# A shorter load list ahead of an attention and state-space kernel: two chunks first, the rest behind the small transfers

## The chip, the cores and the metric

One core of a Trainium2 chip runs the kernel. The metric is the device time of one execution in microseconds. Before the change it was 1209.28 us (median of 3 runs, 1208.81 to 1212.46). The engines named below: PE is TensorE with its weight loads (PEld), DVE is VectorE, ACT is ScalarE, POOL is GpSimd, SP is SyncE, which here only issues DMAs.

## What is computed

Two independent halves, joined along the last axis. A is a state-space convolution (S4) of 576 channels with 128 complex states each, over 2048 positions; B is attention with 32 query heads of 18 columns and a single shared key and value head.

```python
# A: K[d, l] = Re sum_n C[d, n] * exp(dt[d] * A[d, n] * l) * dt[d] * B[d, n]
P = jnp.exp(logdA[:, :, None] * l[None, None, :])
K = jnp.einsum("dn,dnl,dn->dl", Cc, P, dB).real
y = irfft(rfft(pad(u)) * rfft(pad(K)))[..., :L] + u * Dskip
# B: x is [1, 2048, 576], 32 heads of 18
q = (x @ wq).reshape(B, S, H, Dh).transpose(0, 2, 1, 3)
k, v = x @ wk, x @ wv
p = softmax(einsum("bhqd,bkd->bhqk", q, k) * Dh ** -0.5)
out = einsum("bhqk,bkd->bhqd", p, v).reshape(B, S, H * Dh) @ wo
```

## The kernel before

**Attention.** The 2048 positions are four chunks of 512 (`CT`). Keys are used as columns of `kaug` (128 partitions x 2048): for each of two heads a band of 55 rows, the high part of the key twice, its low part between, and a row of ones. Queries of two heads stand the same way in one of five `aug` tiles. One *pair* (line 478, `scores`) is a block of 128 keys against 512 queries of two heads: two matmuls into a score tile `s`, of which three exist. Line 489 takes the exponential of such a tile (128x1024) on ScalarE into one of eight `P` tiles; `product` (line 779) multiplies two of them with the values `v_sb` into `ops`. `main` (line 726) issues pairs in rounds of three (`NS`), all on the order of chunk, group of four heads, block of keys, pair of heads. Pairs 0 to 7 use the keys of chunk 0, 8 to 15 those of chunk 1, and so on; pair 32 is the first of the second group and needs the heads 4 and 5, pair 33 the heads 6 and 7. From the twelfth block of keys on, `force` makes sure that the aug tile of the next group has been asked for.

**Side work.** `side` (line 654) computes the other queries: `qproj` (line 366) for each chunk and each of five column blocks `wq[m]`, its high and low parts stored to DRAM (`qd`) from POOL and fetched from there into aug tiles by SP. `queries` for block 0 of chunk 0 comes first; it stores heads 4 to 7 out of the setup's `keys` tile (`store_first`). `prepare` and the output projections follow for each chunk.

**Convolution.** `Conv` works on 12 chunks of 48 channels. `front(k)` makes the kernel: `arguments` (line 1003) multiplies the parameters `raw` with exp(`dt`), makes the phase f and the exponent m (128x1248 each) and reduces the phase; `factors` (line 1051) takes the sines of f and of |f| (as a cosine) and the exponential of m; `tables` and `kgen` make 2048 positions out of them. Sine and exponential stand in different tables of ScalarE, so each run of sines inside the loop costs two table loads. Such a *burst* is shared by two chunks: the second one's factors go to DRAM (`kept`, tile `fr`) and come back (`restore`). `back(k)` transforms and multiplies. The generators are advanced by a planner with its own clock `K` (estimated times of PE, VectorE and ScalarE): `fill` puts their steps into the gaps of the attention, and `settle` (line 334) sets that clock behind the setup.

**The order.** On PE, ScalarE and VectorE the instructions run in the order in which the program emits them; DMAs go out in the order of emission on each issuing engine. A wait of one instruction therefore holds everything behind it on its engine.

**The setup** (line 222). SP issues dt0 and raw0 (parameters of convolution chunk 0, line 986), wkv, the five loads of chunk 0 of x (`x0`, line 255), then five of 384 or 768 KB for chunks 1 to 3 (`xr`, line 260), and wq1. `conv.begin(n)` advances `front(0)` by n steps. PE projects the queries of 96 columns and the keys of chunk 0 into `first` (line 280); ScalarE copies it (`h1`), VectorE takes the maximum `ab` and the remainder `l1`; SP and POOL place them into kaug and into the first two aug tiles by small transfers of 18 rows. `rest` projects the keys of chunks 1 to 3 and all values. `small`, `kmax`, `aw` and `bias` make the bound that the first group's exponentials subtract (L494 instead of L496).

Of the kernel before, what the change touches and what calls it, by code (L numbers as in the profile page):

```python
# [9 lines left out]
F32 = mybir.dt.float32  # L10
F32R = mybir.dt.float32r
# [173 lines left out]
class Attention:  # L185
# [36 lines left out]
    def setup(self, tp, conv):  # L222
# [13 lines left out]
        wkv = tp.tile([P, 5, 64], F32, name="wkv_sb")  # L236
        xr = tp.tile([P, 5, 3, CT], F32, name="xr")
# [5 lines left out]
        h1, l1, h2, l2, vt = (self.keys[:, j, :] for j in range(5))  # L243
        self.x0 = x0 = self.xp.tile([P, 5, CT], F32, name="x0", tag="x")

        nc.gpsimd.memset(x0[64:, 4, :], 0.0)
        nc.gpsimd.memset(xr[64:, 4], 0.0)
        for j in range(2):
            nc.gpsimd.memset(self.ring[j].bitcast(F32), 0.0)
        conv.early()  # L250
        nc.scalar.dma_start(self.wq[0], a["wq"][0])
        nc.sync.dma_start(wkv, a["wkv"])
        for k in range(5):
            n = DT[k][1]
            nc.sync.dma_start(x0[:n, k, :], a["xT"][0, :n, k, :])
# [8 lines left out]
        self.load_wq(1)  # L264
# [7 lines left out]
        self.todo, self.busy, self.group = [], False, 0  # L272
        self.side_work = Stream(self.side(), self.k, 99.0)
        conv.begin(6)
        p1, small = (self.ps_s.tile([P, 2, CT], F32, tag="s", name=n)[:, 0, :] for n in ("first", "small"))
        p2 = self.bank(CT, "second")
        pv = self.ps_o.tile([P, CT], F32, tag="o", name="vps")

        def queries(ps, j, k):
            nc.tensor.matmul(ps[32 * j:32 * j + 32, :], self.wq[0][:, k, 32 * j:32 * j + 32], x0[:, k, :],  # L280
                             start=(k == 0), stop=(k == 4), tile_position=(0, 32 * j))

        def project(ps, j, i, c, k):
            nc.tensor.matmul(ps[32 * j:32 * j + 32, :], wkv[:, k, i:i + 32], xr[:, k, c - 1, :] if c else x0[:, k, :],
                             start=(k == 0), stop=(k == 4), tile_position=(0, 32 * j))

        def rest(k):
            for c in range(1, NCH):
                project(p2, c - 1, 0, c, k)
            queries(p2, 3, k)  # L290
            for c in range(NCH):
                project(pv, c, 32, c, k)
# [8 lines left out]
        self.place(0, h1, l1, 96, (nc.sync, nc.sync))  # L301
        for pr in range(2):
            for row, src in ((0, h1), (18, h1), (36, l1)):
                for j in range(2):
                    h, b = 2 * pr + j, 64 * j + row
                    q = nc.sync if pr and row == 36 else nc.gpsimd
                    q.dma_start(self.aug[pr][b:b + 18, :].bitcast(F32), src[h * DH:h * DH + DH, :].bitcast(F32))
        V.tensor_scalar(self.km[:, 0:1], ab[:, 0:1], spread[:, 139:140], None, op0=ALU.mult)
        conv.begin(4)
        rest(0)  # L310
        nc.tensor.matmul(small[:, 0:1], spread[:, 0:128], self.km[:, 0:1], start=True, stop=True)
        V.tensor_copy(self.kmax[:, 0:1], small[:, 0:1])
        aw = self.p2.tile([P, P], F32, tag="aw", name="aw_first")
        V.tensor_scalar(aw, ab[:, 0:1].broadcast_to([P, P]), self.kmax[:, 0:1], 1.002, op0=ALU.mult, op1=ALU.mult)
        rest(1)
        matmul4(nc, small[:, 8:12], aw, self.sel[:, 0:4])
        V.tensor_reduce(self.bias, small[:, 8:12], axis=AX.X, op=ALU.max)
        V.tensor_scalar(self.bias, self.bias, -SCALE, None, op0=ALU.mult)
        for k in range(2, 5):
            rest(k)  # L320
        V.tensor_copy(h2, p2)
        V.tensor_tensor(l2, p2, h2.bitcast(F32), op=ALU.subtract)
        self.place(1, h2, l2, 0, (nc.sync, nc.gpsimd))
        V.tensor_copy(vt.bitcast(F32), pv)
        V.tensor_reduce(self.km[:, 4:5], p2, axis=AX.X, op=ALU.max, apply_absolute_value=True)
        self.vt = vt.bitcast(F32)

    def place(self, c, hi, lo, i, qs):
        for row, t in ((0, hi), (36, hi), (18, lo)):
            for j in range(2):  # L330
                b = 64 * j + row
                qs[j].dma_start(self.kaug[b:b + 18, c * CT:(c + 1) * CT].bitcast(F32), t[i:i + 18, :].bitcast(F32))

    def settle(self, conv):
# [3 lines left out]
        h2, l2 = self.keys[:, 2, :], self.keys[:, 3, :]  # L338
        vp = self.bank(CT, "vp").rearrange("p (j n) -> p j n", j=4)
        for j in range(4):  # L340
            nc.tensor.transpose(vp[:, j, :], self.vt[:, j * P:(j + 1) * P], self.ident)
        for src, dst in ((ab[96:, 0:1], ab[96:, 1:2]), (km[96:, 4:5], ab[96:, 0:1]), (ab[96:, 1:2], km[96:, 4:5])):
            V.tensor_copy(dst, src)
# [1137 lines left out]
```

## Time and profile before

| | us |
|---|---|
| median of the runs | 1209.28 |
| the profiled execution | 1208.62 |
| its span | 1206.8 |
| mean granted clock of TensorE | 0.991 |
| first exponential of the attention | 28.39 |
| sine bursts inside the loop | 6 (five of two chunks, one of chunk 11) |

Rows of the timeline read: start, length, engine, line, operation, result<-operands, count, and in brackets the idle time of that engine before it with what ended it. Rows of windows read: stretch, its length, busy time of PE, PEld, DVE, ACT and POOL (with instructions), granted clock of TensorE, busy share of the DMA engines, GB/s. SPq, ACTq and POOLq are the engines' queues as they issue DMAs. PE's matmuls are issued as two instructions each and four row groups run side by side.

### The profile page before, as it was taken

What the parts mean: (1) busy time and instruction counts of PE and PEld (TensorE: products, weight loads), DVE (VectorE), ACT (ScalarE), POOL (GpSimd) and SP (SyncE); (2) the same over time, 40 slices, a digit from 0 to 9 for tenths busy, and PEclk for the clock granted to TensorE, in tenths of its full rate; (3) what the DMA queues carried; (4) which work ended last, traced back from release to release, by engine and by line L of the source; (5) the groups of instructions that cost most, each with busy time, mean ns of one, the idle gap of its engine ahead of it and who ended that gap; (6) DMA issues with size and microseconds to landing.
All of it is one profiled execution on the core that took longest, in us unless ns stands there. A gap on an engine that the chain in (4) does not pass through costs nothing.

```text
span 1206.8 us, 32948 instructions
## 1 busy us (share of the span) xinstructions
PE 1140.2 (94%) x13862; PEld 470.7 (39%) x13862; DVE 978.4 (81%) x1570; ACT 1034.8 (86%) x1090; POOL 129.9 (11%) x233
## 2 busy tenths in 40 slices
PE   6999899999999999989999989999899999999997
PEld 1344333344334434434434333444343444334333
DVE  4766987997887996996886997896998997895833
ACT  3978979888999888999898998889889888998983
POOL 4320401030211000010121000001041000000000
PEclk9999999999999999999999999999999999999999
DMA  7522424023243113133224122113043112012111
GB/s 230 159 75 91 135 96 129 26 73 110 87 151 100 54 35 96 48 97 116 60 92 136 48 94 76 52 55 119 18 147 113 65 36 90 26 53 78 36 41 43
DMA packets 62047, 102.15 MB, mean 85 GB/s; under 512 B 18135, under 2 KB 28999, under 8 KB 61381
## 3 DMA queue, kind: packets, MB, share of 16 engines
q1 hardware_dynamic: 46821, 84.93, 21.2%
q0 software_dynamic: 14496, 14.60, 4.7%
q8 instruction: 111, 1.82, 0.6%
q10 hardware_dynamic: 576, 0.45, 0.1%
q14 instruction: 43, 0.35, 0.1%
HBM read 55.66 MB, written 42.89 MB: 82 GB/s over the span
## 4 chain that ended last, share of the span: by engine, by line
PE 74%; DVE 10%; ACT 9%; issue 4%; DMA 2%; SPq 0%; ACTq 0%; DVEq 0%
PE ops L786 31%; PE s L485 22%; ACT P L496 7%; PE q L380 5%; PE op L182 5%; PE kg L1166 3%; PE iy L182 3%; DVE acc L112 1%; PE hu L182 1%; PE lk L182 1%; DMA xr<-xT 1%; DVE ks L112 1%; PE hk L182 1%; PE lu L182 1%; PE fin L182 1%
## 5 line engine op out<-in xcount | busy, mean ns | idle before, releaser
L496 ACT ACTIVATE P<-s 128x1024 f32<-128x1024 f32 x992 | 937.9, 1030 | 128.5 <-PE s L485 123.9
L786 PE MATMUL ops<-P,v_sb 128*32 128x512 f32 x4096 | 517.7, 600 | 12.3 <-DVE o L116 12.2
L485 PE MATMUL s<-aug,kaug 55*128 55x512 f32 x2048 | 367.2, 444 | 27.4 <-ACT P L496 23.8
L485 PEld LDWEIGHTS s<-aug,kaug 55*128 55x128 f32 x2048 | 169.4, 185 | 339.3 <-ACT P L496 294.2
L786 PEld LDWEIGHTS ops<-P,v_sb 128*32 128x32 f32 x4096 | 113.5, 110 | 163.0 <-issue 120.9
L430 POOL DMA_DIRECT2D qd<-qh x116 | 66.5, 580 | 490.9 <-DVE qh L116 488.4
L182 PE MATMUL op<-wo_sb,oT 126*32 126x288 f32 (+1 forms) x1128 | 81.3, 409 | 3.6 <-DVE ob L116 2.0
L380 PE MATMUL q<-x,wq_sb 128*32 128x256 f32 x1360 | 84.4, 387 | 0.0
L112 DVE TENSOR_TENSOR tab<-tab,tt 128x576 f32<-128x576 f32 (+1 forms) x72 | 59.0, 819 | 1.5
L112 DVE TENSOR_TENSOR tab<-sum,r 128x576 f32<-128x576 f32 (+1 forms) x72 | 58.8, 817 | 0.0
L112 DVE TENSOR_TENSOR tt<-f,sum 128x576 f32<-128x576 f32 (+1 forms) x72 | 58.8, 817 | 0.0
L112 DVE TENSOR_TENSOR tab<-r,dif 128x576 f32<-128x576 f32 (+1 forms) x72 | 58.8, 817 | 0.0
L112 DVE TENSOR_TENSOR tab<-tab 128x576 f32<-128x576 f32 (+1 forms) x72 | 58.8, 816 | 0.0
L380 PEld LDWEIGHTS q<-x,wq_sb 128*32 128x32 f32 x1360 | 41.7, 111 | 41.3 <-issue 18.0
L116 DVE COPY ksb<-kg 128x192 f32<-128x192 f32 x48 | 17.5, 364 | 46.4 <-PE kg L1166 46.2
L182 PEld LDWEIGHTS op<-wo_sb,oT 126*32 126x32 f32 (+1 forms) x1128 | 33.0, 109 | 48.4 <-issue 21.7
L112 DVE TENSOR_TENSOR acc<-acc,pt 128x1728 f32<-128x1728 f32 (+2 forms) x36 | 48.6, 1351 | 0.4
L112 DVE TENSOR_TENSOR pt<-us,ks 128x1728 f32<-128x1728 f32 (+2 forms) x36 | 48.4, 1352 | 0.2
L494 ACT ACTIVATE P<-s,bias 128x1024 f32<-128x1024 f32 x32 | 33.0, 1121 | 14.1 <-PE s L485 14.1
L1166 PEld LDWEIGHTS kg<-tab 128*32 128x32 f32 x2304 | 36.6, 110 | 21.7 <-issue 8.8
L1166 PE MATMUL kg<-tab 128*32 128x64 f32 x2304 | 41.6, 220 | 0.0
L112 DVE TENSOR_TENSOR ks<-ks 128x576 f32<-128x576 f32 (+1 forms) x48 | 41.0, 854 | 0.7
(152 smaller groups left out, 995.1 us busy)
## 6 DMA issues: line engine op xcount, KB each, us to landing
aug<-qd SPq DMA_DIRECT2D x124, 110.0 KB
od<-o SPq DMA_DIRECT2D x31, 256.0 KB
fr<-stage SPq DMA_DIRECT2D x10, 624.0 KB
qd<-qh POOLq DMA_DIRECT2D x24, 216.0 KB, 4.4
u<-u SPq DMA_DIRECT2D x12, 384.0 KB
kd<-ksb SPq DMA_DIRECT2D x12, 384.0 KB
kt<-kd SPq DMA_DIRECT2D x48, 96.0 KB
outa<-u SPq DMA_DIRECT2D x12, 384.0 KB
```

Of the source, the lines that this page charges most:

```text
L112: return self.v.tensor_tensor(out, *a, **k)
L116: return self.v.tensor_copy(out, *a, **k)
L182: nc.tensor.matmul(ps[j:e], w[:, j:e], x, start=start, stop=stop, tile_position=(0, j))
L380: nc.tensor.matmul(ps[o, 256 * f:256 * f + 256], w[:, k, i], xt[:, k, x], start=(k == 0), stop=(k == 4), tile_position=(0, 32 * j))
L430: q.dma_start(qd[h:h + n, row + d:row + d + nd, cs], src[i1:i1 + n * nd, :cs.stop - cs.start].bitcast(F32))
L485: nc.tensor.matmul(ps[:, j, :], self.kaug[r, kb * P:(kb + 1) * P], t[r, :], start=True, stop=True)
L494: nc.scalar.activation(pt, ps, AF.Exp, bias=self.bias, scale=SCALE)
L496: nc.scalar.activation(pt, ps, AF.Exp, scale=SCALE)
L786: nc.tensor.matmul(o_ps[32 * j:32 * j + 32, :], self.v[:, kb, :], pts[2 * n + j // 2][:, j % 2, :], start=(kb == 0), stop=(kb == 15), tile ...
L1166: nc.tensor.matmul(ps[32 * g:32 * g + 32, d, :], t[:, :32], t[:, 32:], start=(j == 0), stop=(j == 1), tile_position=(0, 32 * g))
```

## The change

Setup: SP loads dt0, raw0, wkv and chunk 0 as before, then dt1 and raw1, chunk 1, and two of chunk 2's five pieces. The small transfers of chunk 0's keys and of the first queries follow, and behind them the rest of chunk 2 and chunk 3. wq1 is not loaded in the setup any more. PE projects `first` as before and then only `second`: keys of chunk 1, values of chunks 0 and 1, and the remaining queries.

Keys and values of chunks 2 and 3: `settle` is now called in four rounds. Round 0 places chunk 1's keys and turns the values of chunks 0 and 1; rounds 1 and 2 project chunks 2 and 3 into `third`; at the end of round 2 its parts are taken and placed by twelve transfers on SP, and the setup's pool is given back (`opened`), which issues the DFT matrices, two u and two dsk; round 3 turns the other values, makes `kmax` and loads wq1 to wq4. Until then (`settling`) no side work is started.

Sines: convolution chunks 0 and 1 are now a pair, so are 2 and 3, up to 10 and 11. The sines of chunks 0 and 1 are taken in the setup, ahead of the first exponential; their exponents' products and exponentials follow in the first rounds. Both exp(dt1) and exp(dt0), in this order, stand ahead of the first sine table.

```diff
+        def load(c, ks):
+            for k in ks:
+                n = DT[k][1]
+                nc.sync.dma_start(self.xs[c][:n, k, :], a["xT"][c, :n, k, :])
         conv.early()
         nc.scalar.dma_start(self.wq[0], a["wq"][0])
         nc.sync.dma_start(wkv, a["wkv"])
-        for k in range(5):
-            n = DT[k][1]
-            nc.sync.dma_start(x0[:n, k, :], a["xT"][0, :n, k, :])
+        load(0, range(5))
+        conv.load(1)
         nc.scalar.dma_start(self.sel, a["sel"][:, 0:45])
         nc.scalar.dma_start(spread[:, 0:140], a["sel"][:, 45:185])
-        for k in range(5):
-            n = DT[k][1]
-            nc.sync.dma_start(xr[:n, k], a["xT"][1:4, :n, k, :].rearrange("c p n -> p c n"))
+        load(1, range(5))
+        load(2, range(2))
...
-        self.load_wq(1)
...
         conv.begin(6)
...
         for k in range(5):
-            for j in range(3):
-                queries(p1, j, k)
-            project(p1, 3, 0, 0, k)
+            self.project(p1, k, (("q", 0), ("q", 0), ("q", 0), ("k", 0)))
         nc.scalar.activation(h1, p1, AF.Copy)
...
+        self.place(0, h1, None, 96, nc.sync)
+        heads(0, 0, h1, nc.gpsimd)
+        heads(0, 18, h1, nc.gpsimd)
+        heads(1, 0, h1, nc.scalar)
+        heads(0, 36, l1, nc.gpsimd)
+        self.place(0, None, l1, 96, nc.sync)
+        heads(1, 18, h1, nc.gpsimd)
+        heads(1, 36, l1, nc.sync)
         V.tensor_scalar(self.km[:, 0:1], ab[:, 0:1], spread[:, 139:140], None, op0=ALU.mult)
-        conv.begin(4)
...
+        conv.begin(2)
+        self.p2nd = p2 = self.bank(CT, "second")
+        for k in range(5):
+            self.project(p2, k, (("k", 1), ("v", 0), ("v", 1), ("q", 0)))
+            if k == 0:
+                nc.tensor.matmul(small[:, 0:1], spread[:, 0:128], self.km[:, 0:1], start=True, stop=True)
+                V.tensor_copy(self.kmax[:, 0:1], small[:, 0:1])
...
+                conv.begin(1)
+            if k == 2:
+                matmul4(nc, small[:, 8:12], aw, self.sel[:, 0:4])
...
+        conv.begin(2)
+        load(2, range(2, 5))
+        load(3, range(5))
+        self.split(p2, self.keys[:, 2, :], self.keys[:, 3, :], self.keys[:, 4, :].bitcast(F32), 3)
...
+    def settle(self, n, conv):
...
+        if n == 0:
+            self.place(1, self.keys[:, 2, :], None, 0, nc.sync)
+            self.place(1, None, self.keys[:, 3, :], 0, nc.gpsimd)
+            self.turn_values(self.keys[:, 4, :].bitcast(F32), ((32, 0), (64, 1)))
...
+            conv.begin(3)
+            K.v = K.t + 3.0
...
+        if n in (1, 2):
+            for k in ((0, 1), (2, 3, 4))[n - 1]:
+                self.project(self.p3rd, k, (("k", 2), ("v", 2), ("k", 3), ("v", 3)))
+                K.pe(0.88)
+        if n == 2:
...
+            self.split(self.p3rd, hi, lo, vt, 4)
+            for c, i in ((2, 0), (3, 64)):
+                self.place(c, hi, lo, i, nc.sync)
...
+        if n == 3:
+            self.turn_values(self.vt, ((32, 2), (96, 3)))
...
+            for m in range(1, 5):
+                V.memset(self.wq[m][0:1, 0, 0:1], 0.0)
+                self.load_wq(m)
+            K.pe(2.0)
+            K.v = max(K.v, K.t) + 1.0
+            K.fill = K.v
+            self.settling = False
...
-            if r == 0:
-                self.settle(conv)
+            if r <= 3 * NS:
+                self.settle(r // NS, conv)
+                if r == 2 * NS:
+                    self.opened(conv)
...
-        nc.scalar.activation(dt, dt, AF.Exp)
-        yield "v", K.act(0.25) + 0.2, False
+        if k == 0:
+            nc.scalar.activation(self.raw[1][1], self.raw[1][1], AF.Exp)
+        if k != 1:
+            nc.scalar.activation(dt, dt, AF.Exp)
+            yield "v", K.act(0.25) + 0.2, False
...
         V.tensor_scalar(r.bitcast(I32), f.bitcast(I32), 0x7FFFFFFF, None, op0=ALU.bitwise_and)
+        if k < 2:
+            nc.scalar.activation(f, f, AF.Sin, scale=TWO_PI)
+            if k == 1:
+                nc.scalar.activation(r, r, AF.Sin, scale=-TWO_PI, bias=self.hp)
+        yield "v", 0.0, False
         if k == 0:
-            nc.scalar.activation(f, f, AF.Sin, scale=TWO_PI)
-        yield "v", 0.0, False
-        if k == 0:
-            tt(m, ch(av, NF), row(1), op=mu)
-            yield "v", 0.0, False
+            nc.scalar.activation(r, r, AF.Sin, scale=-TWO_PI, bias=self.hp)
+        if k < 2:
+            self.late.append((ch(av, NF), m))
...
-        both = k % 2 == 1 and k + 1 < NCK
-        if k % 2 == 0 and k > 0:
+        both = k % 2 == 0
+        if not both:
             yield "v", self.kept_ready, False
             f, r = self.kept
...
+            def opened(conv):
+                setup.close()
+                conv.open(ctx)
+                conv.start()
```

`project` issues one step of four matmuls, each with its own weights (queries, keys or values) and its own chunk; `split` takes high part, low part, a plain copy and the maximum on VectorE; `place` copies 18 rows of them into kaug; `turn_values` transposes 128x128 blocks on PE and copies the value columns.

More of the change, by code (lines that the diff above doesn't have):

```diff
@@ L309, in setup @@
-        conv.begin(4)
[L310 to L317, printed above, removed]
@@ L1329, in early @@
         self.load(0)
-        self.n, self.burst = -1, False
+        self.n, self.burst, self.late = -1, False, []
         self.streams = [Stream(self.front(0), self.k)]
@@ L1391, in build @@
         at = Attention(tc, ctx, aps, clock)
+        setup = ExitStack()
         cv = Conv(tc, ctx, at.bank, aps, clock)
```

182 lines of the change are left out of this document (83 added, 99 removed).

## The prediction, made before the changed kernel had run

> **What bounds the kernel now.** I read the page first: its engine table and its shares of the chain.
>
> ```profile
> span 1206.8 us, 32948 instructions
> PE 1140.2 (94%) x13862; PEld 470.7 (39%) x13862; DVE 978.4 (81%) x1570; ACT 1034.8 (86%) x1090; POOL 129.9 (11%) x233
> PE 74%; DVE 10%; ACT 9%; issue 4%; DMA 2%; SPq 0%; ACTq 0%; DVEq 0%
> ```
>
> TensorE is the bound: 67 us idle in all, and three quarters of the chain. Its work is the same after the change (60 projection matmuls before and after, plus four transposes), so the change can act only through PE's idle time and through a lower clock after idle. That idle time lies in two places, read next in the windows (engine sums, then granted clock, DMA share, GB/s): the start, and the windows holding the six sine bursts.
>
> ```profile
> 24.00:48.00 24.00, 20.86 (x176) 8.45 (x172) 18.16 (x39) 18.45 (x18) 10.29 (x21) 0.93 0.54 159
> 144.00:168.00 24.00, 19.06 (x187) 7.46 (x182) 21.65 (x33) 20.04 (x22) 3.50 (x6) 0.90 0.31 102
> 264.00:288.00 24.00, 23.98 (x362) 11.30 (x358) 14.95 (x32) 20.49 (x24) 4.98 (x9) 1.00 0.38 109
> 312.00:336.00 24.00, 21.96 (x214) 8.00 (x214) 22.26 (x30) 21.89 (x23) 7.59 (x13) 0.93 0.36 113
> 504.00:528.00 24.00, 20.30 (x212) 8.03 (x208) 23.69 (x30) 23.57 (x24) 4.98 (x9) 1.00 0.48 151
> 696.00:720.00 24.00, 21.35 (x266) 9.27 (x266) 23.76 (x33) 22.45 (x23) 0.00 (x0) 1.00 0.26 100
> 864.00:888.00 24.00, 18.99 (x244) 8.55 (x238) 22.66 (x31) 19.72 (x19) 7.66 (x14) 0.93 0.28 78
> 1032.00:1056.00 24.00, 21.82 (x224) 8.41 (x216) 23.16 (x32) 22.23 (x24) 0.00 (x0) 1.00 0.10 33
> ```
>
> A quiet window (264 to 288) has no idle time. Then the timeline and the chain of the setup (start, length, engine, operation; in brackets the idle time before it).
>
> ```profile
> 0.75 0.39 SPq L986 DMA_DIRECT2D dt<-ldt  x1
> 4.86 0.24 ACT L1009 ACTIVATE dt<-dt 128x48 f32<-128x48 f32 x1 [0.93 <-DMA dt<-ldt]
> 6.17 0.36 DVE L112 TENSOR_TENSOR raw<-raw,dt 128x192 f32<-128x192 f32 x1 [5.02 <-DMA raw<-prm]
> 6.75 0.59 SPq L255
> 7.62 1.45 DVE L112 TENSOR_TENSOR f<-raw,pos_sb 128x1248 f32<-128x1248 f32 x1
> 9.11 0.81 DVE L120 TENSOR_SCALAR r<-f 128x1248 f32<-128x1248 f32 x1
> 11.45 0.81 DVE L120 TENSOR_SCALAR r<-f 128x1248 int32<-128x1248 int32 x1
> 12.29 1.24 ACT L1036 ACTIVATE f<-f 128x1248 f32<-128x1248 f32 x1 [5.89 <-DVE r L120]
> 13.34 0.61 PE L280 MATMUL first<-x,wq_sb 128*32 128x512 f32 x3
> 13.77 0.61 PE L280 MATMUL first<-x,wq_sb 128*32 128x512 f32 x3
> 14.45 0.60 ACT L297 ACTIVATE keys<-first 128x512 fp32r<-128x512 f32 x1 [0.91 <-PE first L284]
> 15.08 0.69 DVE L124 TENSOR_REDUCE ab<-first 128x1 f32<-128x512 f32 x1 [2.82 <-ACT keys L297]
> 16.29 1.28 ACT L1088 ACT_TABLE_LOAD   x1
> 16.41 1.45 DVE L112 TENSOR_TENSOR m<-raw,pos_sb 128x1248 f32<-128x1248 f32 x1
> 10.18 14.58 DMA xr<-xT
> 24.82 3.80 DMA aug<-keys
> 28.39 3.19 ACT L494 ACTIVATE P<-s,bias 128x1024 f32<-128x1024 f32 x3 [9.26 <-PE s L485]
> ```
>
> The first exponential starts at 28.39, held by xr (three chunks of 576 x 512 f32, 3.5 MB), which the small aug and kaug transfers queue behind. Taking bytes from their path is what would shorten the setup. The question is what is late next.
>
> **The change part by part.**
>
> **A, the start of the exponentials.** The load of dt1 now goes out on SP behind x0's five loads, so at 7.34 (6.75 + 0.59) at the earliest. On ScalarE, exp(dt1) is emitted *ahead* of exp(dt0). Behind it on that engine stand exp(dt0), the sine table, the sine of f, the copy that makes h1, two aug issues and all exponentials; VectorE's first multiply waits for exp(dt0). dt0 took 4.1 us from issue to its exp (0.75 to 4.86) with little ahead of it; I take the same for dt1: 11.5. It can hardly be faster; with x0's megabyte ahead in the queue it may be 12.5. The quickest landing in the table of DMA issues (last number, us) gives the floor, 9.4:
>
> ```profile
> qd<-keys POOLq DMA_DIRECT2D x3, 4.0 KB, 2.0
> ```
>
> The Trainium skill ("DMA: Bandwidth & Descriptors", section "Anatomy of one DMA — SWDGE (gpsimd) path") gives a DMA a fixed cost of some 2.0 us beside its bytes. By that page alone dt1 would be there at an estimated 9.4, and term A would be at its low end; dt0's own row says twice that cost.
>
> From 11.5: two exps of 0.24, VectorE starts at 12.0 instead of 6.17. Its chain to the end of the absolute value takes 6.09 (6.17 to 11.45 + 0.81): 18.1. Sine 1.24: 19.4. Copy 0.60: h1 at 20.0 instead of 15.05. The sine that had 0.9 us to spare ahead of the copy is now 4.5 us late.
>
> From h1 to the first exponential VectorE runs in order: maximum, l1 and km 1.36 (15.05 to 16.41); chunk 1's weights 1.45 (6.17 to 7.62); f2 1.49 (7.62 to 9.11); kmax and aw 0.5; rounding 0.84 (9.11 and the next start 9.95, the difference); bias 0.4; f2-r2 1.5; absolute value 0.81: 8.4. ScalarE then has two sines (2.4, overlapping a little) and the exp table (1.28), all emitted ahead of the exponentials. Together 12.1, so 32.1. Transfers do not hold it: small ones issued from 20 with an almost empty queue need the 3.8 us of the chain plus some 5 us of issues, 29. **A = +3.7**; at dt1's ends +1.6 and +4.7.
>
> **B, projections moved behind the start.** One projection step is two groups 0.43 apart (13.34, 13.77); five steps are 4.3, the four more transposes 0.7. Before, this lay under the xr wait. Now it runs in rounds 1 to 3, with idle time of PE from 28.39 to 48 as cover: of the 3.1 in the window from 24 to 48 I take half, the rest being the xr waits before 28.39. **B = 5.0 - 1.5 = +3.5**; 0 if ScalarE's rounds hide it all (the two exps of m, 2.5 us, now also stand among them), 5.0 if nothing does.
>
> **C, the second query weights.** wq1 was loaded in the setup. Now it is issued in round 3, on SP behind chunk 2's and 3's twelve kaug transfers, the DFT matrices, two u and two dsk.
>
> ```profile
> 28.67 6.79 SPq L332 DMA_DIRECT2D kaug<-keys  x9
> 42.94 0.13 PEld L380 LDWEIGHTS q<-x,wq_sb 128*32 128x32 f32 x4 [0.30 <-issue]
> u<-u SPq DMA_DIRECT2D x12, 384.0 KB
> dft_sb<-dft SPq DMA_DIRECT2D x1, 1024.0 KB
> 47.00:48.00 1.00, 1.00 (x18) 0.26 (x8) 1.00 (x3) 1.00 (x2) 0.00 (x0) 1.00 0.93 354
> 150.86 1.06 PE L786 MATMUL ops<-P,v_sb 128*32 128x512 f32 x8 [4.07 <-DVE o L116]
> 151.00:154.00 3.00, 3.00 (x18) 0.97 (x17) 3.00 (x3) 1.33 (x2) 0.00 (x0) 0.66 0.79 249
> 154.00:157.00 3.00, 3.00 (x22) 0.88 (x14) 2.96 (x4) 1.74 (x3) 0.00 (x0) 0.77 0.93 377
> ```
>
> Counted from the first exponential (P0): the third projection ends about P0 + 10.2 (three rounds of 3.2 and what stands between), its high part is there at 10.9. Twelve issues at 0.75 (6.79 / 9): 19.9. Five loads, 2.4: wq1 goes out at 22.3. Ahead of it from 20.4 are 1.84 MB of dft and u and some 0.2 of dsk, then its own 0.33: at 354 GB/s 6.7 us, 27.1, and about 1.4 to land: 28.5. The q matmuls of unit (0,1) came 14.5 us after P0 (42.94). Side work is now held until round 3, and the planner's margin behind it is 3 us less: I put them at P0 + 21.5, about 18 pairs in. From pair 24 on they are forced, at P0 + 26, so some wait is likely in any case. TensorE then stands 7 us in its queue, with the next scores and products behind it, ScalarE running dry after three pairs. The wait at 150.86 shows what follows one: 4.07 us idle, then 3 us each at 0.66 and 0.77, together 1.7 us lost; less 1.2 because the planner may have placed some filler earlier. **C = +7.5**; 0 and +12 as ends (wq1 in time; a 10 us wait and the clock).
>
> **D, one burst fewer.** Chunks 0 and 1 pair in the setup; the five pairs left replace five pairs and a single. Idle plus clock loss per window above (1 less the clock, times 24): 4.9 + 2.4, 2.0 + 1.7, 3.7, 2.7, 5.0 + 1.7, 2.2: 26.3. The four middle ones average 4.2, five of them 21.0: **D = -5.3**. At 2.65 each it is -13; at 6.7 each +7.
>
> The Trainium skill ("ScalarE: Activation LUTs", section "What ACT_TABLE_LOAD costs") says that a change of table costs the 1.28 us load and a drain of 1.38.
>
> ```profile
> 146.69 1.28 ACT L496 ACT_TABLE_LOAD   x1
> 147.98 1.94 ACT L496 ACTIVATE P<-s 128x1024 f32<-128x1024 f32 x2
> ```
>
> The trace has the next exponential 1.29 after the load's start and no drain. By the page the dropped burst would free 5.3 us of ScalarE and A be 1.4 larger; by the trace 2.6, and I go by it.
>
> **At nothing.** The stores of heads 4 to 7 start after round 3; pair 32 is the first to need them. Chunk 1's kernel factors go through DRAM ahead of chunk 0's tables: some 9 us later for the first convolution chunk, covered by attention, which outlasts the convolution by 50 us:
>
> ```profile
> 1154.63 1.44 PE iy L182 x32
> ```
>
> If it does not catch up, those products end later in that cover. Chunk 1's kaug rows, issued behind the late loads from about 30, land by 35 and are due at pair 8, 40.
>
> **Sum.** 3.7 + 3.5 + 7.5 - 5.3 = +9.4, on the profiled execution's 1208.62 (1.8 beside its span; 0.7 under the median 1209.28): **1218**.
>
> **The rivals.**
> Rival 1, *no wait for wq1*: the q matmuls come late enough, or the DMAs run faster. For it: DMA share is only 0.54 in 24 to 48. Against: forcing at pair 24. +9.4 - 7.5: 1210.5.
> Rival 2, *the bursts decide, faster than before*: with the first one gone (7.3 us in 144 to 168) the rest could cost as little as that of 696, 2.65: -13. Without a wait for wq1, 3.7 + 3.5 - 13 = -5.8: 1202.8. It decides as soon as the five cost under 3.8 each (26.3 - 7.2, over 5) with C at 0. Against: two of the four middle ones cost 3.7, one 6.7.
> Rival 3, *the setup does get shorter*: dt1 there when dt0 is, h1 at 15.05, P0 at 27.2, A = -1.2: 1213.1. Against: the SP row at 6.75.
> Rival 4, *one wait more*: unit (0,1) late, its queries reach aug only after pair 33 needs them. Behind a late wq1 the queries still pass three VectorE steps, the store to DRAM and the fetch from it, two landings like dt0's 4.1 us, while pair 33 is some 12 pairs off. I put 5 us on it: 1223.
>
> **How the numbers follow.** Forecast 0.50, rivals 0.15, 0.12, 0.10, 0.13. A measurement here tells apart 0.3%, 3.6 us: 1205.7 to 1212.9. Faster: rival 2 and a little of rival 1, 0.14. Same: the rest of rival 1 and a little of rival 3, 0.15. Slower 0.71. All low ends together would give 1197, all high ones 1237; they will not meet. Range 1207 to 1229: rival 2 and the worst of rival 4 stay out, 0.2 in all. The forecast's own is 1214 to 1223.
>
> **What would show it.** A: exp(dt) waiting for a DMA until 9.4 to 12.5, the copy of h1 released by the sine, a first exponential at 30 to 33. B: matmuls on "third" in the first three rounds. C: a q matmul on PE released by the DMA into wq_sb, several us long, some 20 us after P0, and a low clock behind it. D: ten table loads in the loop for twelve, one more ahead of the first exponential. I am wrong if the first exponential starts before 28, if no PE wait names wq_sb, or if the five bursts cost under 13 or over 30 us.

## The result, and the profile after

The changed kernel takes 1222.3 us (median of 4 runs, 1220.86 to 1222.64) against 1209.69 us of the kernel before beside it (4 runs, 1208.81 to 1212.46). The ratio is 1.0098, with the interval from 1.0079 to 1.0117. The profiled execution took 1220.86 us, span 1219.1, mean granted clock 0.983.

The page of the changed kernel, engine table and shares of the chain:

```profile
PE 1144.7 (94%) x13866; PEld 470.3 (39%) x13866; DVE 980.2 (80%) x1577; ACT 1032.4 (85%) x1088; POOL 129.4 (11%) x232
PE 62%; DVE 22%; ACT 8%; issue 4%; DMA 3%; SPq 0%; DVEq 0%; ACTq 0%
```

The engines have the same work as before. TensorE is idle for 74.4 us of the span instead of 66.6, and the same work keeps it busy 4.5 us longer, at a mean clock of 0.983 instead of 0.991: together the 12.3 us by which the spans differ. What moved is the chain: VectorE holds 22% of it instead of 10, and TensorE 62 instead of 74. Next the setup in the timeline of the changed kernel (start, length, engine, operation; in brackets the idle time and what ended it):

```profile
7.41 0.57 SPq L1016 DMA_DIRECT2D dt<-ldt  x1
8.51 10.01 SPq L256 DMA_DIRECT2D xr<-xT  x15
11.82 0.24 ACT L1040 ACTIVATE dt<-dt 128x48 f32<-128x48 f32 x1 [7.88 <-DMA dt<-ldt]
19.50 0.58 ACT L282 ACTIVATE keys<-first 128x512 fp32r<-128x512 f32 x1
32.25 6.14 ACT L522 ACTIVATE P<-s,bias 128x1024 f32<-128x1024 f32 x6
```

The rows show the wait of 7.88 us for dt1, the first query copy (h1) at 19.50 instead of 14.45, and the first exponential (P0) at 32.25 instead of 28.39. All fifteen loads of chunks 1 to 3 went out in one run from 8.51, although eight of them are emitted behind the small transfers: those had to wait for h1, the loads did not. SP's order is thus not that of the program, against what is said of the order above, and "the rest behind the small transfers" was not in force in this kernel.

The rounds behind it, same view of the same kernel:

```profile
36.15 2.88 PE L322 MATMUL third<-xr,wkv_sb 128*32 128x512 f32 x16
40.73 2.76 PE L322 MATMUL third<-xr,wkv_sb 128*32 128x512 f32 x24
54.85 2.69 SPq L220 DMA_DIRECT2D wq_sb<-wq  x4
57.63 1.15 SPq L1129 DMA_DIRECT2D fr<-stage  x2
62.76 1.93 PE L408 MATMUL q<-x,wq_sb 128*32 128x256 f32 x32
67.40 0.36 DVE L116 COPY tab<-r 128x384 f32<-128x384 f32 x1 [4.92 <-DMA fr<-stage]
75.62 0.38 PE L182 MATMUL up<-sel_sb,aw 128*32 128x8 f32 x16 [5.23 <-DVE aw L120]
76.83 3.12 ACT L522 ACTIVATE P<-s,bias 128x1024 f32<-128x1024 f32 x3 [8.43 <-PE s L513]
```

No instruction waits for wq_sb. VectorE waits 4.92 us at 67.40 for the store of convolution chunk 1's factors, because the first table is written where those factors stood (`stage` and `tab` share a buffer). Behind the tables on VectorE stand the queries of unit (0,1) (qh at 73.15, then aw); TensorE waits 5.23 us for aw with its next scores in the queue, and ScalarE stands dry for 8.43 us.

Windows of the kernel before, then of the changed one (engine sums, granted clock, DMA share, GB/s):

```profile
24.00:96.00 72.00, 68.06 (x848) 28.71 (x848) 46.05 (x86) 57.12 (x59) 26.53 (x50) 0.98 0.42 121
96.00:216.00 120.00, 111.49 (x1320) 45.51 (x1324) 101.77 (x169) 106.64 (x113) 17.79 (x30) 0.97 0.33 107
```

```profile
24.00:48.00 24.00, 19.20 (x129) 6.70 (x117) 13.38 (x30) 18.29 (x17) 9.53 (x18) 0.78 0.30 68
24.00:96.00 72.00, 61.48 (x632) 24.25 (x620) 44.29 (x85) 48.56 (x48) 20.76 (x38) 0.85 0.44 128
96.00:216.00 120.00, 118.56 (x1524) 50.09 (x1528) 105.44 (x179) 106.34 (x115) 17.33 (x30) 1.00 0.32 97
```

I call idle time of TensorE plus (1 less the clock) times the length the *loss* of a stretch, as the prediction did for the bursts. From 24 to 96 us it is 3.9 + 1.4 = 5.4 before and 10.5 + 10.8 = 21.3 after: +15.9. From 96 to 216 it is 12.1 before, with the first burst at 140.55, and 1.4 after, where that burst is gone: -10.7. The end of the first and of the 31st of the 32 groups of heads (VectorE's copy of the products) shows the same, in the kernel before and in the changed one:

```profile
70.71 0.69 DVE L116 COPY o<-ops 128x512 f32<-128x512 f32 x1 [1.35 <-PE ops L786]
...
1158.91 0.69 DVE L116 COPY o<-ops 128x512 f32<-128x512 f32 x1 [2.22 <-PE ops L786]
```

```profile
89.75 0.68 DVE L116 COPY o<-ops 128x512 f32<-128x512 f32 x1
...
1171.01 0.69 DVE L116 COPY o<-ops 128x512 f32<-128x512 f32 x1 [2.22 <-PE ops L814]
```

The first group is 19.0 us late, the 31st 12.1: the opening costs 19, and all that follows gives back 7.

Last the bursts: windows from 2 us ahead of each burst's first table load to 34 us behind it, of the kernel before (six bursts) and of the changed one (five); the rows left out have a clock of 1.00, the last row sums all.

```profile
138.55:174.55 36.00, 30.03 (x296) 12.21 (x300) 33.29 (x50) 31.37 (x33) 4.08 (x7) 0.91 0.39 127
...
877.87:913.87 36.00, 33.33 (x414) 13.77 (x406) 34.20 (x59) 33.94 (x36) 13.91 (x24) 0.98 0.43 131
...
sum 216.00, PE 193.68 PEld 77.88 DVE 203.65 ACT 198.64 POOL 32.10; mean PE 32.28 PEld 12.98 DVE 33.94 ACT 33.11 POOL 5.35
```

```profile
235.37:271.37 36.00, 34.29 (x428) 14.56 (x418) 33.66 (x55) 32.50 (x34) 10.53 (x19) 0.99 0.37 116
...
626.25:662.25 36.00, 30.49 (x262) 10.29 (x250) 28.64 (x40) 33.74 (x36) 3.51 (x6) 0.95 0.34 112
793.67:829.67 36.00, 31.40 (x294) 11.67 (x286) 34.68 (x47) 32.06 (x33) 0.00 (x0) 0.95 0.17 64
...
sum 180.00, PE 161.30 PEld 62.72 DVE 167.01 ACT 163.06 POOL 14.04; mean PE 32.26 PEld 12.54 DVE 33.40 ACT 32.61 POOL 2.81
```

Before: 22.3 idle and 4.0 of clock, 26.3. After: 18.7 and 4.0, 22.7. The five are 3.6 us cheaper than the six, and single ones range from 2.1 (at 235) to 7.3 (at 626).

### The profile page after: what moved, and what is told of

The parts are those of the page before. It is cut to its first block, busy times and chain, and to the rows that moved or that the text cites. A ratio compares the mean times of both kernels' runs of the same rounds, so it can differ in the third digit from the quotient of the medians.

```text
span 1219.1 us, 32963 instructions
## 1 busy us (share of the span) xinstructions
PE 1144.7 (94%) x13866; PEld 470.3 (39%) x13866; DVE 980.2 (80%) x1577; ACT 1032.4 (85%) x1088; POOL 129.4 (11%) x232
## 4 chain that ended last, share of the span: by engine, by line
PE 62%; DVE 22%; ACT 8%; issue 4%; DMA 3%; SPq 0%; DVEq 0%; ACTq 0%
PE ops L814 26%; PE s L513 18%; ACT P L524 7%; DVE tab L112 4%; PE op L182 4%; DVE acc L112 3%; PE q L408 3%; DVE ks L112 3%; PE kg L1199 3%; PE iy L182 2%; DVE pt L112 2%; DVE stage L112 2%; PE hu L182 1%; PE lu L182 1%; PE lk L182 1%
## 5 line engine op out<-in xcount | busy, mean ns | idle before, releaser
L493 POOL DMA_DIRECT2D qd<-sh x20 | 12.9, 643 | 400.9 <-DVE sh L120 353.2
L112 DVE TENSOR_TENSOR u<-u,iy 128x384 f32<-128x384 f32 x24 | 13.3, 554 | 47.6 <-PE iy L182 47.4
```

The source lines that it names most:

```text
L112: return self.v.tensor_tensor(out, *a, **k)
L493: nc.gpsimd.dma_start(qd[h0 + n0:h1, 54, :].rearrange("p (a n) -> p a n", a=2), two(sh, h1 - h0 - n0))
```

## The experiments

Twelve kernels were run. Each is compared with the kernel before, run beside it on the same chip (medians 1210.5 to 1211.5 in the later comparisons). "First group" is the delay of its end against 70.71 in the kernel before.

**Own exponential first.** The changed kernel with exp(dt0) emitted ahead of exp(dt1).

```diff
-        if k == 0:
-            nc.scalar.activation(self.raw[1][1], self.raw[1][1], AF.Exp)
         if k != 1:
             nc.scalar.activation(dt, dt, AF.Exp)
+            if k == 0:
+                nc.scalar.activation(self.raw[1][1], self.raw[1][1], AF.Exp)
```

> Only two instructions on ScalarE change places: exp(dt0) ahead of exp(dt1). Theory (term A, the wait of exp(dt1) for its DMA delays the whole setup): VectorE's first multiply at 6.2 us instead of 12.2, the copy of h1 at 14 to 15 instead of 19.5, the first exponential at 27 to 28 instead of 32.25, and the whole execution 4 to 5 us shorter than the changed kernel, 1217 to 1218.5. Rival (the start is not on the path, what follows waits for DMAs anyway): the first exponential moves, the total by less than 1.5 us.

Measured: 1217.22 us, ratio 1.0053 [1.0035, 1.0070]. Its timeline:

```profile
4.72 0.24 ACT L1040 ACTIVATE dt<-dt 128x48 f32<-128x48 f32 x1 [0.79 <-DMA dt<-ldt]
27.07 3.12 ACT L522 ACTIVATE P<-s,bias 128x1024 f32<-128x1024 f32 x3
73.72 3.12 ACT L522 ACTIVATE P<-s,bias 128x1024 f32<-128x1024 f32 x3 [10.04 <-PE s L513]
```

P0 comes 5.2 us earlier than in the changed kernel, and the median falls by 5.1 (an estimate of 2 to 8 us, from the two ratios with their intervals). That the order of the two exponentials costs time at the end is shown. That it reaches the end in full is not, and that 5.2 and 5.1 agree is chance: in the profiled executions the first group ends 2.6 us earlier than in the changed kernel (87.18 against 89.75) and the span is 2.1 us shorter (1217.0 against 1219.1). VectorE's wait for the store rises from 4.92 to 7.05 us and takes part of the early start; the hole of ScalarE stays, and is even longer.

**The convolution's loads later.** The DFT matrices and the first u and dsk issued in round 8 instead of with `opened` in round 2, so that wq1 and the store of chunk 1's factors stand ahead of them on SP.

```diff
             def opened(conv):
                 setup.close()
                 conv.open(ctx)
-                conv.start()
...
+            if r == 24:
+                conv.start()
```

> The loads of the DFT matrices and of u are issued in round 8 instead of round 2, so that the store of chunk 1's factors is not behind 1.8 MB. Theory (the hole in the first group is VectorE waiting 4.9 us for that store, with the query work behind it): that wait goes, the 8.4 us hole of ScalarE near 77 us shrinks under 3, and the execution is 5 us shorter than the changed kernel (3.5 to 7): about 1217. Rival (TensorE would have waited for something else): the hole moves, total within 1.5 us of the changed kernel.

Measured: 1218.37 us, ratio 1.0065 [1.0047, 1.0082], 3.9 us less than the changed kernel, by the two intervals only just a difference. The first group ends 3.0 us earlier (86.75). VectorE's wait for the store fell from 4.92 to 1.53 us and ScalarE's hole from 8.43 to 5.37. That the hole would go altogether was wrong: TensorE still waits 2.5 us for aw.

**Both.**

> Both edits together. Theory (two separate losses one after the other): they add, 9 to 10 us shorter than the changed kernel, 1212 to 1214. Rival (they overlap, one hides the other): not more than the better of the two alone, about 1217.

Measured: 1212.54 us (12 runs, 1209.6 to 1215.76), ratio 1.0019 [1.0007, 1.0031]; 9.8 us less than the changed kernel, against 5.1 + 3.9 of the two alone. The totals add, as far as the intervals can tell. The first group gains 8.5 us (it ends at 81.25), more than the 2.6 and 3.0 of the two alone: an early start is worth its whole only when it is not spent waiting for the store. What is left in its first group (+10.5 us):

```profile
58.05 0.36 DVE L116 COPY tab<-r 128x384 f32<-128x384 f32 x1 [1.67 <-DMA fr<-stage]
66.84 0.31 PE L182 MATMUL up<-sel_sb,aw 128*32 128x8 f32 x16 [2.54 <-DVE aw L120]
67.67 3.13 ACT L522 ACTIVATE P<-s,bias 128x1024 f32<-128x1024 f32 x3 [5.36 <-PE s L513]
77.41 0.96 PE L513 MATMUL s<-aug,kaug 55*128 55x512 f32 x5 [1.31 <-DMA aug<-qd]
```

VectorE still waits 1.67 us for the store, but TensorE's 2.54 us for aw are now the length of the queries' own four steps on VectorE. The wait on aug, for the queries of pair 33, is the one that rival 4 of the prediction named, at 1.3 us instead of 5; in the changed kernel itself nothing waits for aug there.

**wq1 in the setup.** The changed kernel with wq1 loaded behind the five and two early loads, wq2 to wq4 in round 3.

```diff
         load(2, range(2))
+        self.load_wq(1)
...
-            for m in range(1, 5):
+            for m in range(2, 5):
```

> The second query weights are loaded in the setup again, ahead of the small transfers. Theory of the prediction's term C (the q matmuls wait for them): 5 us or more shorter than the changed kernel, 1217 or less. Rival, from the trace after (no wait names these weights, the hole has another cause): no change, within 1.5 us, 1221 to 1224.

Measured: 1224.16 us, ratio 1.0105 [1.0085, 1.0124]. No gain. ScalarE's hole is 12.65 us, VectorE's wait for the store 8.68. The q matmuls come at 61.37, 29.1 us after P0 instead of 30.5, so wq1 was not what they waited for.

**Loads and keys only.** The attention of the changed kernel with the convolution of the one before (one chunk's sines in the setup, six bursts).

```diff
-        conv.load(1)
...
-        both = k % 2 == 0
-        if not both:
+        both = k % 2 == 1 and k + 1 < NCK
+        if k % 2 == 0 and k > 0:
```

> The attention's part of the change alone (two chunks first, keys and values of chunks 2 and 3 in the first rounds, side work held until round 3); the convolution as before, with one chunk's sines in the setup and six bursts in the loop. Theory (term B and what comes with it is a real loss, the bursts a real gain): the first exponential at 24 to 26, but the first group of heads ends 3 to 8 us later than in the kernel before, nothing is gained later, 1213 to 1218. Rival (all of the loss came from the sines ahead of the exponentials and from the store of the factors): the first group ends as early as before or earlier, 1205 to 1211.

Measured: 1224.72 us, ratio 1.0118 [1.0095, 1.0141], worse than either theory had it. Its timeline:

```profile
22.05 1.11 ACT L520 ACTIVATE P<-s,bias 128x1024 f32<-128x1024 f32 x1 [1.48 <-PE s L511]
26.25 5.20 PE L321 MATMUL third<-xr,wkv_sb 128*32 128x512 f32 x16
27.85 0.28 PEld L321 LDWEIGHTS third<-xr,wkv_sb 128*32 128x32 f32 x8 [1.42 <-DMA xr<-xT]
79.87 0.69 DVE L116 COPY o<-ops 128x512 f32<-128x512 f32 x1 [2.38 <-PE ops L812]
```

The exponentials start 6.3 us before those of the kernel before and the first group still ends 9.2 us after. The projections of chunks 2 and 3 take 5.20 us here for the sixteen instructions that take 2.88 in the changed kernel. Part of that is the load list itself: in this kernel seven loads do go out behind the small transfers (from 21.93), as the change meant, and the weight loads of the projection wait 2.0 us for them (1.42 in the row above and 0.58 more). The window shows the rest:

```profile
26.00:32.00 6.00, 6.00 (x22) 1.13 (x20) 2.82 (x4) 2.56 (x4) 3.61 (x8) 0.56 0.75 243
```

TensorE counts as busy throughout, at a clock of 0.56. The late queries leave a hole of ScalarE of 5.28 us, as above. An early start alone was worth nothing; the work that the setup had hidden came up behind it. How much of the 9.2 us is the projections and how much the held queries isn't parted by this kernel.

**Sines only.** The attention, loads and projections of the kernel before with the sines of two chunks in the setup, own exponential first, and the convolution's loads in round 8.

```diff
+            if r == 24:
+                conv.start()
...
-        both = k % 2 == 1 and k + 1 < NCK
+        both = k % 2 == 0
```

> The convolution's part of the change alone (pairs 0 and 1 to 10 and 11, five bursts), with exp(dt0) ahead of exp(dt1) and the loads of the DFT matrices and of u in round 8, on the attention, loads and projections of the kernel before. Theory (term D: fewer bursts gain, here with the sines under the wait for xr): the first exponential within 1.5 us of 28.4, the first group at most 4 us late, and 5 to 10 us gained behind it: 1200 to 1207, faster than both kernels. Rival (what was gained behind the first group in the changed kernel was only held work caught up): 1208 to 1213.

Measured: 1217.3 us, ratio 1.0055 [1.0035, 1.0075]; neither range held it. The first exponential comes at 30.78, 2.4 us late where 1.5 was allowed. Here nothing holds the queries until round 3 and TensorE's "up" waits for nothing, but pair 33's queries come late into aug:

```profile
75.58 1.64 PE L488 MATMUL s<-aug,kaug 55*128 55x512 f32 x5 [4.00 <-DMA aug<-qd]
76.46 2.85 ACT L499 ACTIVATE P<-s 128x1024 f32<-128x1024 f32 x3 [5.45 <-PE s L488]
```

I took the tables on VectorE, which stand among the steps of these queries, for the cause; the third kernel of the next experiment shows that they are not. The first group ends 12.0 us late, the fifth 0.5 us early, the 31st 6.1 late: the missing burst gives back what the opening cost, and the later bursts take some again.

**Tables later.** If chunk 0's tables stand in the queries' way on VectorE, they can be moved behind them: the planner's due time for chunk 1's stored factors, 30 us instead of 9, in the changed kernel, in the one with both repairs and in the one with the sines alone.

```diff
-            self.stored = K.t + 9.0
+            self.stored = K.t + (9.0 if k else 30.0)
```

> The changed kernel with one number altered: the due time of chunk 1's stored factors 30 us instead of 9 behind their issue, so that VectorE is given other work before the table that must wait for the store. Nothing on the queues moves. Theory: the 4.92 us wait of VectorE for the store is what opened the 8.43 us hole; with the query work ahead of the tables the hole falls to under 4 us, VectorE's wait on the store is under 1 us and the time is 1216 to 1219, as much as the later DFT loads gave (1218.4) or more. Rival: the hole comes from the queries being held to round 3; it stays over 6 us with another releaser, and the time is 1220 to 1224.

> Own exponential first and the convolution's loads at round 8, as in the kernel with both changes (1212.5 us), and beside it the planner's due time of the stored factors of chunk 1 raised from 9 to 30 us, so that chunk 0's tables are emitted behind the query work. Theory: what was left of the wait of TensorE's small product on VectorE's aw (2.5 us there) and of the queries' way to pair 33 (1.3 us and the 3.6 us hole of ScalarE beside it) came from these tables; both go, no hole of ScalarE over 3 us stands in the first group, and the time is 1207 to 1210. Rival: the queries' chain (projection in round 3, three VectorE steps, store, fetch) is itself too long for pair 33, the wait on aug stays at 1 us or more, and the time is 1211 to 1215.

> The kernel with the sines alone (1217.3 us: attention of before, sines of two chunks in the setup) with the due time of the stored factors at 30 us instead of 9. Theory: the 4.0 us wait for pair 33's queries, which stood behind chunk 0's tables on VectorE, goes; the first group's delay falls from 12 to 8 us or less and the time is 1211 to 1214. Rival: the first group does gain, but the groups behind it take it back as in the kernel with the sines alone, and the time is 1216 to 1219.

Measured: 1236.31 us, ratio 1.0207 [1.0185, 1.0229]; 1229.38, 1.0157 [1.0137, 1.0177]; 1227.43, 1.0142 [1.0117, 1.0166]. All three lost 10 to 17 us, which no expectation allowed. Rows of the first:

```profile
74.04 3.12 ACT L522 ACTIVATE P<-s,bias 128x1024 f32<-128x1024 f32 x3 [5.36 <-PE s L513]
83.57 1.64 PE L513 MATMUL s<-aug,kaug 55*128 55x512 f32 x5 [2.83 <-DMA aug<-qd]
94.71 0.35 DVE L116 COPY tab<-r 128x384 f32<-128x384 f32 x1
```

VectorE's wait for the store is gone and the hole falls to 5.36, so some 3 of its 8.43 us were the store's; the rest stands with the late queries, which then make pair 33 wait, and the first group ends no earlier (91.63 against 89.75). The first table comes at 94.71 instead of 67.40, and the loss shows at the bursts: with both repairs, the losses of the five windows, taken as above, sum to 21.1 us with the due time of 9 and to 33.1 with 30, 12 of the 17 us.

Rows of the third, the kernel with the sines alone and its tables later, and one window of it:

```profile
63.21 0.60 POOL L468 DMA_DIRECT2D qd<-sh  x1 [0.15 <-issue]
71.69 2.69 SPq L477 DMA_DIRECT2D aug<-qd  x7
74.01 1.65 PE L488 MATMUL s<-aug,kaug 55*128 55x512 f32 x5 [4.33 <-DMA aug<-qd]
61.00:69.00 8.00, 7.81 (x96) 3.18 (x88) 0.00 (x0) 7.18 (x8) 2.66 (x5) 1.00 0.95 300
```

The tables are gone from the first group (the first comes at 85.36) and VectorE has nothing to do from 61 to 69, yet TensorE waits 4.33 us for aug where it waited 4.00. The last store of these queries is issued at 63.21 and their fetch only at 71.69, 8.5 us later. With the sines alone the two are 7.6 us apart (65.64 and 73.20), with both repairs 4.2 (70.80 and 75.01). In the two slow cases the DFT matrices and u, 1.8 MB that round 8 issues, go out just ahead of the store (from 59.41, and from 62.69), and the DMA engines are 95% busy behind them (91% from 64 to 70 with the sines alone). So the tables are ruled out, and the rows point to the later loads, one of the two repairs, which meet the queries' store here; no kernel moved those loads once more to show it by itself.

**The same delay in the kernel before.** Is it the delay itself, or the new pairing?

```diff
         self.fac = r, f, sm, df
+        if k == 0:
+            self.stored = K.t + 26.0
```

> The kernel before, with one addition: chunk 0's tables are given a due time 26 us behind the sums of its factors, as the due time of 30 us did in the kernels with the sines of two chunks (first table at 42.1 us in the kernel before, 67.4 in the changed one, 84.7 and 94.7 in the two with 30 us). Theory: TensorE's filler is convolution work, so a convolution that starts some 20 us later costs at the bursts in any arrangement, and the time is 1218 to 1228. Rival: attention outlasts the convolution by some 50 us, as the prediction has it, and covers the delay; what cost in the other kernels was the pairing of chunks 0 and 1, and the time is 1207 to 1213.

Measured: 1239.2 us, ratio 1.0224 [1.0209, 1.0238], more than the theory's range. First table, the burst at 938 with what waits behind it, and the last of the convolution's products, in the timeline of this kernel:

```profile
74.57 0.35 DVE L116 COPY tab<-r 128x384 f32<-128x384 f32 x1
...
944.30 1.28 ACT L496 ACT_TABLE_LOAD   x1
945.59 4.69 ACT L496 ACTIVATE P<-s 128x1024 f32<-128x1024 f32 x5
946.67 2.63 PE L485 MATMUL s<-aug,kaug 55*128 55x512 f32 x6 [6.99 <-ACT P L496]
954.52 3.64 PE L786 MATMUL ops<-P,v_sb 128*32 128x512 f32 x16 [5.23 <-DVE o L116]
...
1213.15 2.23 PE L182 MATMUL iy<-w,dft_sb 128*32 128x192 f32 x32 [0.67 <-DVE u L112]
```

and the window of that burst:

```profile
936.16:972.16 36.00, 23.52 (x266) 8.91 (x262) 25.54 (x37) 26.94 (x28) 0.00 (x0) 0.76 0.15 58
```

Two things cost here: a burst, and the end. One burst loses 12.5 + 8.6 = 21.1 us: TensorE waits 6.99 us for exponentials behind the sines and 5.23 for the copy of the products, which stands on VectorE behind the multiplications of the burst's factors; the clock over the window is 0.76. And the last products of the convolution come at 1213, 59 us later than in the kernel before, where 32 us of delay went in. Up to the 24th group there was no loss at all (906.69 against 914.42). The attention's last exponential starts at 1197.91, 11.3 us later than before (1186.60); the span is 30.6 us longer, so 19.3 us fall behind it, where TensorE stands idle for 9.55 us until 1209.70 for VectorE's convolution work. So a delay is neither covered nor paid at once: it shifts the bursts to other places, and here it grew until the convolution outlasted the attention.

**Products in round 1.** The kernel with both repairs, with the products of chunk 1's sines and the store in round 1, where VectorE was idle, instead of round 3; then all four products there.

```diff
         if n == 1:
+            while not hasattr(conv, "kept"):
+                conv.begin(1)
             self.p3rd = self.bank(CT, "third")
```

```diff
+            conv.begin(2)
             self.p3rd = self.bank(CT, "third")
```

> Both repairs (own exponential first, convolution's loads at round 8: 1212.5 us) and the products of chunk 1's sines with their exponentials, with the store of the factors behind them, emitted in round 1, where VectorE stood idle from 30.6 to 39.0 us, instead of round 3 (44.5 us). Theory: the store leaves some 9 us earlier, chunk 0's first table comes at 48 to 54 us instead of 58.1, VectorE's wait of 1.7 us for the store goes, and by the loss of 15 to 17 us for some 25 us of later tables the time is 1206 to 1210. Rival: the third projection's high part, now behind three products on VectorE, comes later by 1 to 3 us, the queries with it, and the time is 1212 to 1216.

> As the run before, with all four products of sines and exponentials in round 1. Theory: as there, with the first table another 1 to 2 us earlier; 1205 to 1210. Rival: one more product of 1.45 us stands ahead of the third projection's high part, keys of chunks 2 and 3 come later still, and the time is 1213 to 1217.

Measured: 1220.13 us, ratio 1.0078 [1.0062, 1.0094], and 1228.67, ratio 1.0142 [1.0127, 1.0158]. The first table did come earlier, at 50.95 and 53.05 instead of 58.05, and VectorE waits for no store; the theory's time was still missed, by 10 us and more. In the first the opening was no worse than in the kernel with both repairs (first group +9.1 against +10.5), so its loss lies behind it. In the second ScalarE stood dry for 7.09 us at 50.45 already, and the first group was 12.2 us late. An earlier convolution did not pay either: that rule of mine, so many us of loss for so many of delay, falls with these two.

## Why the prediction came out as it did

**A, the start.** Right in mechanism and size. The exp waited for dt1 until 11.82 (11.5 foretold), P0 came at 32.25 (32.1), and undoing the order put P0 at 27.07, ahead of the old one; the total gave 5.1 us back by the medians and 2.1 by the profiled executions, around the term. (By its own figures the sine is 4.9 us late at 19.4 against 14.45, not 4.5; nothing hangs on it.) The Trainium skill ("DMA: Bandwidth & Descriptors", section "Anatomy of one DMA — SWDGE (gpsimd) path") has a fixed cost of some 2.0 us for a DMA issued from GpSimd. dt1 goes out on SP, and from its issue to its use the trace has 4.4 (7.41 to 11.82), so the duration of dt0 was the better measure.

**B, the projections.** They ran in rounds 1 to 3, as foretold. From 24 to 48 us the loss is 4.8 + 5.3 = 10.1 against 3.1 + 1.7 = 4.8 before, +5.3 where 3.5 was set. That stretch also holds the later P0, so B and A aren't parted in it. With an early P0 the same stretch loses as much: 2.7 + 6.7 = 9.4 in the kernel with the loads and keys only (clock 0.72), 3.0 + 6.7 = 9.7 in the one with both repairs (0.72). So the loss lies near the term's high end of 5.0, if all of it is the projections', which no kernel parts from the rest of that stretch.

**C, the second query weights.** The step that failed is the wait of TensorE for wq1: no wait names wq_sb, one of the prediction's own signs of being wrong, and loading wq1 early gained nothing. What stands in its place is next to it. The queries were held until round 3 and forced late, as the prediction had it, and TensorE did stand in its queue with ScalarE dry behind it; but it waited for VectorE's aw. The q matmuls came at P0 + 30.5, not 21.5, and found the weights there; with wq1 loaded in the setup they came hardly earlier (P0 + 29.1), so the weights did not set their time. Of ScalarE's hole of 8.43 us some 5.4 remain wherever the queries are held (5.37, 5.36, 5.28 and 5.36 in four kernels); the kernel with the sines alone, which doesn't hold them, has no wait for aw (its hole of 5.45 is that for aug).

**At nothing.** This step failed: the store of chunk 1's factors was costed at nothing because only the convolution would wait for it. It is in the chain, since its wait stands on VectorE ahead of the query work; taking the loads ahead of it away gave 3.9 us. The convolution's first table came at 67.40 instead of 42.13, 25 us later and not 9. And the cover of 50 us was misread: it ran to the end of the span, while the attention's last exponential starts at 1186.60, only 32 us behind the last products at 1154.6; and 32 us of delay in the kernel before cost 28.

**D, one burst fewer.** Ten table loads in the loop, as foretold, and 3.6 us gained by windows of 36 us, where 5.3 was set. That a burst cost 22.7 over 5 = 4.5 us where 4.2 was set is luck. The prediction's slices of 24 us cut the bursts: the one at 332.47 has only its first 3.5 us in the slice from 312 to 336. By the windows set at the bursts, the four middle ones of the kernel before cost 2.4, 4.3, 3.6 and 3.4, on average 3.4; five of those would have gained 9.2, so the five that were left became dearer. What the cost of a burst can't be is a constant: it goes from 2 to 21 us in the runs here. The Trainium skill ("ScalarE: Activation LUTs", section "What ACT_TABLE_LOAD costs") has a drain of 1.38 us beside the load of 1.28; the row at 945.59 begins 1.29 after the load's start, as in the kernel before, and the load begins 0.02 after the last sine ends, so no drain shows on either side of it.

**The sum.** 1218 was foretold and 1222.3 measured; +9.4 was set, and the spans differ by 12.3. By the end of the first group A, B and C were to cost 14.7; it was 19.0. What follows was to give 5.3 back and gave 6.9, of which 3.6 in the burst windows. So the total is right with the help of luck: A is right in its mechanism, B is in the right place and larger, D is near by an accident of its slices, and C priced a wait that does not exist, while the store and the late queries cost about as much in its stead. Rival 1's condition held, no wait for wq1, but not its time of 1210.5, since another wait stood in the same place. Rival 2 fails, since the five bursts cost 4.5 each and not under 3.8. Rival 4's wait for aug is not in the changed kernel. Rival 3 fails: P0 was not early. With its order restored P0 was, at 27.07, but the kernel was slower all the same.

**What stays open.** No version beat the kernel before; the best, both repairs, is 1.0019 [1.0007, 1.0031]. Its first group is 10.5 us late with P0 1.7 early. The held queries were not released earlier in any kernel with the new load list, so how much of it they cost isn't shown. Where the later losses of the kernels with other table times come from was traced to a single burst and the end in one kernel only; for the two with the products in round 1 it is not known. All of this rests on one trace of each kernel, and two executions of one kernel differ by up to 9 us here (1233.26 to 1242.06 in the changed kernel with the tables later), so single differences of 2 or 3 us are not more than hints.

## What to carry to other kernels

Before a transfer is costed at nothing, look whose instruction waits for its buffer and what stands behind that instruction on its engine: here a store to DRAM held a copy, the copy held the queries, and the queries held TensorE. Work taken out of the setup pays only if what it had hidden has a cover of its own; an early first exponential (22.05) was lost again within one group of heads. A load that is moved out of one transfer's way can meet another: with the sines alone, the loads of round 8 went out just ahead of the queries' store, and it took 7.6 us from its issue to the fetch instead of 4.2. Where filler is placed by a planner, moving one due time moves every later burst, so a difference of a few us behind the opening is no verdict on the part that was changed.

## What was not expected of the hardware

SP sent the loads that are emitted behind the small transfers ahead of them: fifteen in one run of 10.01 us from 8.51, and the six kaug transfers only behind h1, from 20.61. With h1 at 14.84, in the kernel with its own exponential first, nine loads went out ahead of them (5.52 us from 8.50) and six behind. This need not be the chip's doing: the kernel fixes the order by hand for TensorE, ScalarE and VectorE alone (`manual_schedule`), and no run tells whether the build or the chip put SP's loads ahead.

The clock was low in the opening rounds even while TensorE was busy: 0.56 over six busy microseconds in the kernel with the loads and keys only, behind six (20 to 26) with 1.8 us idle and a clock of 0.87, and 0.78 over the changed kernel's whole window from 24 to 48, in which 4.8 us are idle. What work costs there follows it: sixteen projection matmuls took 2.88 us from 36.15, and twenty-four took 2.76 from 40.73, where the clock was 0.73 (36 to 40) and 1.00 (40 to 44).
